# Loading k and q of the first 512 tokens by head halves, eight tokens to a partition, over two DMA rings

## The chip, the cores and the metric

The kernel runs on one core of a Trainium2 chip. The metric is the device time of one execution in microseconds (us). The core has TensorE (PE) with its weight loads (PEld), VectorE (DVE), ScalarE (ACT), GpSimd (POOL) and SyncE (SP). PE writes to PSUM alone; ACT and DVE empty PSUM; POOL works on SBUF. DMAs are put on a ring by the engine that issues them and run on 16 DMA engines.

## The reference

There are 8 sequences of 576 tokens, 8 heads of 64. Attention sees a band of 32 tokens on each side; its result is the input of a feed-forward network with a squared ReLU.

```
scores = (q @ k.T) / sqrt(64);  scores = where(|i - j| <= 32, scores, -1e9)
attn   = exp(scores - max) ;    attn = attn / (sum + 1e-9)
x      = (attn @ v), heads side by side, reshaped to (4608, 512)
h      = x @ w_in                      # 512 -> 2048
out    = (s * max(h, 0)**2 + b) @ w_out  # 2048 -> 512, float32
```

All inputs are float32. The kernel casts to bfloat16 ahead of the matmuls.

## The kernel before, in words

**Tiles.** The 4608 tokens are 36 tiles of 128. Tile j attends with its 128 queries as two halves of 64, each against 128 keys, so it needs key blocks j and j+1, where block j starts 32 tokens ahead of query tile j. The feed-forward part takes 8 tiles of 128 tokens and then 14 of 256: `s1` (L1114, x by w_in), a ReLU on ACT (L1124, sometimes DVE), a square on DVE (L1144), `s2` (L1178, by w_out), and an output step on DVE (L1187) that also adds the constant vector CVEC, which needs all of w_out (`cvec`, L1007: matmuls of L1011, a spread of L1023, a DVE step of L1028).

**How k and q come in, up to tile 13.** `load_pair` (L608) fetches 256 tokens of k or q in one DMA (two where a sequence ends inside): two tokens to a partition, all 8 heads, so that a contiguous piece is 2 x 64 floats, 512 bytes. K0 is a special case: it starts 32 tokens ahead of the data, so it has 112 partitions, and the first 16 are set to zero by a DVE memset (L462). `cast_pair` (L634) turns it to bfloat16 in KQN in two instructions of 128x512. `turn_pair` (L645) transposes it on PE in two groups of four 128x128 transposes into a PSUM bank (L653; profile names tp and ht) and then copies it to KQT, one copy of 128x512 for each tile (recorded as L597 on ACT, L592 on DVE, the lines of the helper `move`). v is loaded by `load` (L566) in pieces of 256 bytes. w_in and w_out are loaded by `load_w` (L536) in four parts each of 1 MB with pieces of 2 KB, into the buffer that later holds GT (so the profile calls it gt), and cast in four instructions each.

**Attention of one tile.** `attend` (L881): 16 score matmuls of 64 rows (L910) into the two banks SC; eight DVE instructions that add the mask and take the maximum (L920); eight exponentials on ACT (L927); the sum's reciprocal on DVE (L935, L938); eight scalings on ACT, DVE or POOL (L593, L598); transposes (L961, for tiles 0 to 3, on PE; by DMA from tile 4 on); the product with v (L983 and others), and a copy to XT.

**What sets the order.** Nothing is ordered by hand but the first loads. A planner (`_Plan.order`, L152) takes each instruction with a key (its due time, from the tile number plus the table RANK), a cost and its dependences, and lays them out on the five engines; it also chooses the engine where several may do it. What it gives is one fixed list for each engine, with semaphore waits. Where it sees PE idle for over 0.3 us in the opening, it puts in fill matmuls on a tile of ones (L500), whose results nobody reads. The constants START to TURN, PAIR and the cost arguments describe the chip to the planner; changing one changes the lists and not the computation. The first loads are listed by hand:

```
FIRST = "K0 Q0 v0 v1 K1 v2 Q1 v3 i0 i1 i2 i3|v4 K2 o0 o1 o2 o3 s0||"   # L68
```

K, Q: pairs; v: one tile; i, o: a quarter of w_in, w_out; s: the two scalars. The part behind the first bar is issued with tile 1. All of it goes by SyncE's ring, in this order; K2 waits for the casts of K0, whose buffer it uses, and each part of w_out for the casts of the w_in part in the same place.

Of the kernel before, what the change touches and what calls it, by code (L numbers as in the profile page):

```python
# [6 lines left out]
BF16 = mybir.dt.bfloat16  # L7
# [5 lines left out]
D = 64  # L13
H = 8
# [10 lines left out]
START, RAMP, RING, ISSUE, LAND, TURN = 800.0, 1200.0, 2700.0, 700.0, 1400.0, 300.0  # L25
# [8 lines left out]
    "av": (-1120, -880, -20, -160, 640, -880, 420, -3660, -2360, -760, 40, 180, 660, 80, -800),  # L34
    "ck": (0, 62940, 0, 63660, 200, 63640, -1120, 63760, 680, 61500, -240, -4080, 400, -3060, 740),
    "cq": (-680, -17980, -1560, -19380, -40, -16220, -760, -24200, -1480, -18720, -1600, -15700, -160, -16880, -740),
    "cs": (60, 460, -6260, -6260, -6260, -6260, -6260, -6260, -6260, -6260, -6260, -6260, -6260, -6260, 0),
    "cv": (-180, -1420, -740, -1220, -1380, -1880, -1340, -640, 4900, -1480, 5600, -300, -940, -420, -1000),
    "ex": (-480, 320, 440, -2400, -220, -240, 20, -180, -220, -1140, 1040, -160, 80, 100, -40),
    "kt": (-340, -29820, 40, -30840, 20, -29740, 2280, -30920, 2000, -31040, -1620, -31040, -3100, -30900, -240),  # L40
    "ktc": (2800, -1080, 820, -420, 300, -740, -200, 1680, 160, 200, -240, -940, 180, -680, 80),
    "ktd": (2020, 2020, 2020, 2020, 2020, 2020, 2020, 2020, 2020, -840, 1240, 100, -4360, -300, -12200),
    "mx": (-460, 100, -380, 0, 2760, -160, 4840, -500, 2280, -140, -80, 300, -640, 260, 3360),
    "no": (-1180, 1780, 200, -1160, 1500, 80, -460, -200, 160, 200, 20, 7880, 2680, -960, -180),
    "ou": (-20, 920, 0, 540, 1380, 920, 1040, 160, 540, -10560, -40, -4920, 560, -5040, 200),
    "pt": (-160, -180, 400, 900, -39920, -39920, -39920, -39920, -39920, -39920, -39920, -39920, -39940, -39940, -60),
    "ptc": (-80, 4280, 1920, -40, -20820, -20820, -20820, -20820, -20820, -20820, -20820, -20820, -21020, -21020, 0),
    "ptd": (70520, 70520, 70520, 70520, 1160, -440, -40, -220, -1960, -1320, -160, -200, -720, -400, -60),
    "qt": (-20, -580, -660, -1700, -80, -2220, -80, -2700, -300, 1000, -10980, 1000, -1240, 680, -320),
    "qtc": (500, 1220, 4440, -720, -20, -260, 740, -3260, -180, -300, -200, -120, 0, 320, 0),  # L50
    "rc": (-560, -720, 240, 180, 120, 500, -1220, -1380, -5320, -880, 300, -540, -3260, 640, 6120),
    "re": (460, 1700, -1680, -4400, -1680, -1760, -3280, 60, 20, -248640, -440, -255780, -480, -255860, -1260),
    "s1": (800, 1520, 420, 4120, -140, -60, -1100, 0, 1600, 12880, 140, 11300, -6540, 11520, -980),
    "s2": (-3780, -700, -20, 40, 1280, -1020, -240, -420, 100, 86620, -8420, 86900, -4240, 86820, 0),
    "sc": (100, 520, -2480, -80, -360, -400, -840, -100, 1400, -1700, -260, -580, -80, 1500, -4320),
    "sq": (360, -540, 1080, 280, 180, -1240, 5280, -160, -60, -1420, 200, 1500, 540, 1500, 780),
    "vo": (28460, 28360, 1180, 540, -80, 2920, 5080, -1540, 260, -80, -1260, 680, -620, -120, 2820),
    "wi": (1180, -11800, -11800, -11800, -11800, -11800, -11800, -11800, -11800, -11800, -11800, -11800, -11760, -11760, 0),
    "wo": (-960, 4060, 4060, 4060, 4060, 4060, 4060, 4060, 4060, 4060, 4060, 4060, 3720, 3720, 0),
    "xt": (840, 100, -100, -520, -1120, 420, -460, 1420, 100, -20, 120, -640, 580, -1000, -220),  # L60
# [5 lines left out]
NPM, SQPOOL, NWHOLE, NV = 0, 0, 4, 5  # L66
PAIR0, FORE, PTB = 16, 2, 5
FIRST = "K0 Q0 v0 v1 K1 v2 Q1 v3 i0 i1 i2 i3|v4 K2 o0 o1 o2 o3 s0||"  # L68
# [42 lines left out]
class _Plan:  # L111
# [40 lines left out]
    def order(self):  # L152
# [15 lines left out]
        dma_free = {"sp": RAMP, "act": 0.0}  # L168
# [15 lines left out]
        while len(out) < len(self.nodes):  # L184
# [65 lines left out]
            if n.dsem is None:  # L250
                end = free[e] + n.lat
            else:
                early, ring = t < STEADY, "act" if e == "act" else "sp"
                if e == "sp":
                    free[e] = room(free[e], n.ndesc)
                took = n.dtime * (1.0 if early else DSLOW)
                dma_free[ring] = max(dma_free[ring], free[e] + (ISSUE if early else n.iss)) + took
                if ring == "sp" and early:
                    dma_free[ring] += TURN if (n.ndesc == 512) != (kind == 512) else 0.0
                    kind = n.ndesc  # L260
                end = dma_free[ring] + (LAND if early else 1000.0)
                if e == "sp":
                    queue.append((dma_free[ring], took, n.ndesc))
                    del queue[:-12]
# [87 lines left out]
def bass_sliding_window_symmetric__then__act_starrelu_kernel(  # L352
# [41 lines left out]
    with ExitStack() as es:  # L394
# [39 lines left out]
        XQ = [sb((128, DM), BF16, "xq") for _ in range(2)]  # L434
        MB = {m: sb((128, 4, 128), BF16, "mb") for m in ("mm", "fm")}
# [22 lines left out]
        K0 = -1.0e6  # L458
        add("dve", lambda e: e.memset(ONES[:], 1.0), 150, K0, writes=["ONES"])
        add("dve", lambda e: e.memset(FLAT[:, 0, :], NEG), 100, K0, writes=[("FLAT", 0)])  # L460
        add("dve", lambda e: e.memset(FLAT[:, 1, :], 0.0), 100, K0, writes=[("FLAT", 1)])
        add("dve", lambda e: e.memset(KALL[0:16, 0:2 * DM], 0.0), 970, K0 + 10, writes=[("K32", 0, "lo")])  # L462
# [16 lines left out]
        if NPM:  # L479
            for m in ("mm", "fm"):  # L480
                add("pool" if m == "mm" else "act", lambda e, m=m: (e.tensor_copy if m == "mm" else e.copy)(
                    MB[m][:, :, :], mm[:, :].unsqueeze(1).broadcast_to((128, 4, 128))),
                    620 if m == "mm" else 550, KC + 2, reads=mids, writes=[("MB", m)])
            add("dve", lambda e: e.memset(MB["fm"][0:64, :, 0:32], NEG), 130, KC + 2, writes=[("MB", "fm")])
        for m, cuts in (("fm", ((0, 0),)), ("ml", ((1, 32),)), ("lf", ((0, 96), (1, 64)))):
            key = KC + 2 if m == "fm" and not NPM else -LEAD
# [23 lines left out]
        lastload = [None]  # L510
        wcnt = [0]
# [24 lines left out]
        def load_w(which, c):  # L536
            if which in WCAST:
# [6 lines left out]
                   else w_out[:, 4 * c:4 * c + 4, :])  # L544
            lastload[0] = add("sp", lambda e: [e.dma_start(w32, src)], 500, -LEAD - 900,
                              writes=[("W32", s_, g) for g in range(4)], dsem=f"dw{s_}",
                              dtime=2800, behind=lastload[0], ndesc=512)
# [18 lines left out]
        def load(src, t0, dst, name, key, sem, x):  # L566
            pcs = parts(t0)

            def fn(e):
                return [e.dma_start(dst[r:r + n, :].rearrange("p (h d) -> p h d", h=H),  # L570
                                    src[b, :, s0:s0 + n, :].rearrange("h s d -> s h d"))
                        for (b, s0, r, n) in pcs]
# [4 lines left out]
            lastload[0] = add("sp", fn, 640.0 * len(pcs), key, writes=[name], dsem=sem,  # L577
                              ndma=len(pcs), dtime=(1040.0 if x < 4 else 1330.0) * tot / 128, behind=lastload[0], ndesc=8 * tot,
                              after=hold + ([gate] if gate and gate.eng == "pe" else []))
            recent.append(lastload[0])  # L580
            if gate and gate.eng == "sp":
# [26 lines left out]
        def load_pair(what, J):  # L608
# [9 lines left out]
            def fn(e):  # L618
# [8 lines left out]
            lastload[0] = add("sp", fn, 640.0 * len(pcs), 128 * j - LEAD - 600, writes=[(nm, 2 * a), (nm, 2 * a + 1)],  # L627
                              dsem=f"d{what}{a}", ndma=len(pcs), dtime=PAIR * tot / 256, behind=lastload[0],
                              ndesc=4 * tot, after=hold + ([gate] if gate and gate.eng == "pe" else []))
            recent.append(lastload[0])  # L630
            if gate and gate.eng == "sp":
# [13 lines left out]
        def turn_pair(what, J):  # L645
# [13 lines left out]
            for x in range(2):  # L659
# [7 lines left out]
                     akey(j) - (128 if what == "K" else 0) + rank(ck_, j), [res], [("KT" if what == "K" else "QT", kt)],  # L667
                     scale=SCALE if what == "Q" and j < NPM else None, after=[first] if first else [])
# [29 lines left out]
        def k_turn(j):  # L698
            kn, kt = j % NB, j % NKT
            key = akey(j) - 128  # L700
            if j > KQDMA:
                add("sp", lambda e: [e.dma_start_transpose(KQT[kt][:, :, :], KQN[kn][:, :])],
                    1300, key + 64 + rank("ktd", j), reads=[("KN", kn), ("QN", kn)],
                    writes=[("KT", kt), ("QT", kt)], dsem=f"dkt{kt}", dtime=1270, ndesc=1024, iss=-316.0)
                return

            def fn(e):
                for pr in range(NPAIR):
# [5 lines left out]
                 key + rank("ktc", j), ["TP"], [("KT", kt)])  # L714
# [26 lines left out]

        def early(j):
            key = akey(j)
            ka, kb = j % NKT, (j + 1) % NKT
            va, vb = VE[j % NVE], VE[(j + 1) % NVE]
            vres = [("VE", j % NVE), ("VE", (j + 1) % NVE)]
            pb, mb, ptb, xq = j % NP, j % NM, j % NPT, j % 2
            kind = "fm" if 2 * j % UPB == 0 else "mm"
            assert kind == "fm" or (2 * j + 1) % UPB < UPB - 1 and 2 * j % UPB < UPB - 1

            def half(blk, pr, a):
                return ((NKT - 1 - blk) * 2 * NPAIR + pr) * 2 + a

            for hh in range(2):
                r0 = 64 * hh
                m = add("pe", lambda e, hh=hh: e.matmul(SC[hh][:, :, :], lhsT=IDENT[:, :], rhs=MB[kind][:, :, :],
                                                        start=True, stop=False),
                        214, key - 150 + rank("mk", j), reads=["IDENT", ("MB", kind)], writes=[("SC", hh)])

                def scores(e, hh=hh, r0=r0):  # L760
                    for pr in range(NPAIR):
                        for u in range(2):
                            c1, c2 = half(kb, pr, 0), half(ka, pr, 1)
                            for part in range(2 if u and c1 > c2 else 1):
                                dst = SC[hh][64 * u:64 * u + 64, pr, :]
                                if u == 0:
# [487 lines left out]
```

## Time and profile before

| | us |
|---|---|
| median of 3 runs (lowest, highest) | 319.09 (317.71, 319.47) |
| the profiled execution, its own time | 318.41 |
| its span, first to last instruction | 316.7 |
| PE busy in the span | 300.6 |
| of it, fill matmuls (L500), first 72 us | 13.35 |
| the first score matmul starts (tile 0) | 9.06 |
| casts of K0 / Q0 start | 4.99 / 7.03 |
| first cast of w_in / the first s1 matmul | 17.90 / 19.36 |
| cast of K2 | 31.78 |
| first cast of w_out / the first s2 matmul | 34.00 / 35.97 |
| matmuls for CVEC start (L1011) | 45.03 |

All times in the lower part are counted from the start of the span. The clock granted to TensorE was 1.00 throughout. A time in the table says when an instruction started; a cast starts when its DMA has landed, or later where the engine is busy.

How to read the rows that are shown further on. A row of the slices gives the busy share of an engine in each fortieth of the span, 7.9 us, in tenths. A row of the chain in order of time has start, length, engine, what was done, and how many. A row of the windows has the window, its length, the busy time and the number of instructions of each engine, the granted clock, the mean busy share of the 16 DMA engines (it can be over 1 where packets overlap), and GB/s.

### The profile page before, as it was taken

The page shows a single profiled execution, that of the slowest core. Times are in us where ns is not written, and L with a number is a line of the kernel's source. Part 1 is how long each engine was busy: PE and PEld are TensorE (multiplying, and loading weights), DVE is VectorE, ACT ScalarE, POOL GpSimd, SP SyncE. Part 2 cuts the span into 40 slices and gives each one's busy share as a digit, 9 for nine tenths or more (in the row PEclk, how much of TensorE's full clock was granted, in tenths as well). Part 3 has the DMA queues.
Part 4 walks back from the last instruction along what each step waited for, and adds up shares of the span by engine and source line. Part 5 has one row for each costly group of instructions (what it writes and reads, how often), then busy time and mean ns, then how long its engine had stood idle before and what let it go on. Part 6 is the DMA issues. An engine that isn't in the chain of part 4 may idle for free.

```text
span 316.7 us, 10629 instructions
## 1 busy us (share of the span) xinstructions
PE 300.6 (95%) x4057; PEld 212.7 (67%) x4095; DVE 214.0 (68%) x930; ACT 218.6 (69%) x767; POOL 181.4 (57%) x393
## 2 busy tenths in 40 slices
PE   6879899999999999999999999999999999999996
PEld 4567675677866776575767676666767585848664
DVE  4786866867977778368497766867777668534432
ACT  4898867988995879278577868686859587706230
POOL 3444455897879475925949676666766771700000
PEclk9999999999999999999999999999999999999999
DMA  8999999999999999996999999999999952310001
GB/s 187 289 404 273 393 193 237 234 212 246 189 169 246 233 180 239 226 224 159 192 181 243 207 198 229 195 203 196 222 193 219 183 135 70 85 51 33 35 35 66
DMA packets 165139, 60.99 MB, mean 193 GB/s; under 512 B 142048, under 2 KB 156512, under 8 KB 165088
## 3 DMA queue, kind: packets, MB, share of 16 engines
q1 hardware_dynamic: 165088, 60.31, 91.2%
q8 instruction: 32, 0.52, 0.7%
q14 instruction: 19, 0.16, 0.2%
HBM read 36.70 MB, written 9.44 MB: 146 GB/s over the span
## 4 chain that ended last, share of the span: by engine, by line
PE 81%; DMA 8%; SPq 4%; ACT 3%; issue 2%; DVE 1%; POOL 1%
PE ht L1114 27%; PE outp L1178 24%; PE tp L1178 10%; PE outp L1114 5%; PE tp L1114 4%; DMA gt<-in_moe_w_in_dram 3%; DMA k<-in_k_dram 3%; PE av L1178 2%; PE av L855 2%; DMA q<-in_q_dram 2%; SPq L619 2%; SPq L570 2%; PE sc L910 2%; PE av L725 2%; ACT p L927 1%
## 5 line engine op out<-in xcount | busy, mean ns | idle before, releaser
L593 POOL TENSOR_SCALAR p<-p,rc 128x128 bf16<-128x128 bf16 x271 | 111.2, 431 | 43.4 <-DVE rc L938 43.4
L927 ACT ACTIVATE p<-ss,mx 128x128 bf16<-128x128 f32 x288 | 111.9, 391 | 23.4 <-DVE mx L920 23.2
L1114 PE MATMUL ht<-xt,win 128*128 128x256 bf16 (+1 forms) x1144 | 109.3, 249 | 1.8 <-DVE mx L920 1.1
L1144 DVE TENSOR_TENSOR gt<-r 128x512 bf16<-128x512 bf16 x144 | 70.3, 490 | 50.6 <-ACT r L1124 48.8
L1114 PEld LDWEIGHTS ht<-xt,win 128*128 128x128 bf16 x1144 | 91.2, 98 | 17.0 <-POOL win L592 1.3
L1124 ACT ACTIVATE r<-ht 128x512 bf16<-128x512 f32 x109 | 64.5, 593 | 44.0 <-PE ht L1114 43.6
L1178 PE MATMUL outp<-wout,gt 128*128 128x512 bf16 (+1 forms) x358 | 83.1, 374 | 3.6 <-issue 2.1
L920 DVE CUSTOM_DVE_ANT_0 ss<-sc,mask 128x128 f32<-128x128 f32 x224 | 52.5, 282 | 12.3 <-PE sc L910 12.3
L1178 PEld LDWEIGHTS outp<-wout,gt 128*128 128x128 bf16 x384 | 35.7, 98 | 37.0 <-DVE cvec L1028 0.6
L927 ACT ACTIVATION_READ_ACCUMULATOR p<-ss,mx 128x1 f32 x288 | 54.4, 189 | 0.0
L1178 PE MATMUL tp<-wout,gt 128*128 128x512 bf16 x136 | 31.3, 379 | 0.9 <-issue 0.5
L592 POOL CAST ve<-v 128x512 bf16<-128x512 f32 x37 | 23.5, 636 | 13.2 <-DMA v<-in_v_dram 12.6
L592 POOL CAST kqn<-k 128x512 bf16<-128x512 f32 x33 | 20.4, 627 | 18.1 <-DMA k<-in_k_dram 18.0
L592 POOL CAST kqn<-q 128x512 bf16<-128x512 f32 x31 | 20.6, 672 | 10.5 <-DMA q<-in_q_dram 10.4
L1187 DVE SCALAR_TENSOR_TENSOR outs<-outp,scb,cvec 128x512 f32<-128x512 f32 (+1 forms) x24 | 17.7, 737 | 12.9 <-PE outp L1178 12.7
L1178 PEld LDWEIGHTS tp<-wout,gt 128*128 128x128 bf16 x144 | 13.6, 98 | 15.6 <-DVE gt L1144 0.2
L920 DVE DVE_READ_ACCUMULATOR2_ANT mx<- 128x1 f32 x288 | 23.4, 81 | 0.0
L592 DVE CAST xt<-av 128x512 bf16<-128x512 f32 (+1 forms) x34 | 22.2, 675 | 1.7 <-PE av L725 1.3
L1114 PE MATMUL outp<-xt,win 128*128 128x256 bf16 x144 | 18.7, 273 | 0.0
L1124 ACT ACTIVATE r<-outp 128x512 bf16<-128x512 f32 x18 | 10.7, 596 | 8.4 <-PE outp L1114 8.4
L1114 PEld LDWEIGHTS outp<-xt,win 128*128 128x128 bf16 x144 | 14.0, 98 | 2.6
L1114 PE MATMUL tp<-xt,win 128*128 128x256 bf16 x120 | 15.6, 273 | 0.0
(84 smaller groups left out, 252.0 us busy)
## 6 DMA issues: line engine op xcount, KB each, us to landing
out_dram<-outs SPq DMA_DIRECT2D x35, 256.0 KB, 2.6
v<-in_v_dram SPq DMA_DIRECT2D x28, 256.0 KB, 4.8
q<-in_q_dram SPq DMA_DIRECT2D x22, 256.0 KB, 4.6
k<-in_k_dram SPq DMA_DIRECT2D x18, 256.0 KB, 4.0
gt<-in_moe_w_in_dram SPq DMA_DIRECT2D x4, 1024.0 KB, 10.4
gt<-in_moe_w_out_dram SPq DMA_DIRECT2D x4, 1024.0 KB, 10.8
q<-in_q_dram SPq DMA_DIRECT2D x4, 512.0 KB, 6.3
v<-in_v_dram SPq DMA_DIRECT2D x8, 192.0 KB, 4.6
```

Source lines behind the costliest of these rows:

```text
L570: return [e.dma_start(dst[r:r + n, :].rearrange("p (h d) -> p h d", h=H), src[b, :, s0:s0 + n, :].rearrange("h s d -> s h d")) for (b, s0, ...
L592: return e.tensor_copy(dst, src)
L593: return e.tensor_scalar(dst, src, scale, 1.0, ALU.mult, ALU.mult)
L619: return [e.dma_start(big[r:r + n // 2, 2 * DM * a:2 * DM * a + 2 * DM].rearrange("p (h x) -> p h x", h=H), src[b, :, s0:s0 + n, :].rearra ...
L725: r = e.matmul(PA[64 * hh:64 * hh + 64, u, 64 * pr:64 * pr + 64], lhsT=vt[r0:r0 + 64, 128 * pr + 64 * hh:128 * pr + 64 * hh + 64], rhs=PTS ...
L920: lambda e, ss=ss, x=x, y=y: e.tensor_tensor_reduce(out=SS[ss][:, x, :], in0=banks[y % 2][0][:, y // 2, :], in1=MASK[kind][:, :], scale=-S ...
L927: lambda e, ss=ss, x=x, y=y: e.activation(P[pb][:, y, :], SS[ss][:, x, :], AF.Exp, bias=MX[mb][:, y:y + 1], scale=-1.0, accum_out=SM[mb][: ...
L1114: r = e.matmul(hbank[:, nt * f:nt * f + nt], lhsT=WIN[:, kc, 128 * ft:128 * ft + 128], rhs=XT[:, kc, x0:x0 + nt], start=(kc == 0), stop=(k ...
L1124: return e.activation(R1[rb][:, :], hbank[:, :], AF.Relu, bias=0.0, scale=1.0)
L1144: return e.tensor_tensor(d, r, r, ALU.mult)
L1178: r = e.matmul(op_[:, 0:cn], lhsT=GT[:, g_, fc, :], rhs=WOUT[:, fc, c0:c0 + cn], start=(fc == 0), stop=(fc == 15))
L1187: add("dve", lambda e, ob=ob, op_=op_, c0=c0, cn=cn: e.scalar_tensor_tensor(OUTS[ob][:, 0:cn], op_[:, 0:cn], SCB[:, 0:1], CVEC[:, c0:c0 + cn],
```

## The change

1. `load_oct`, `cast_oct` and `turn_oct` are new and take the place of K0, Q0, K1 and Q1. `load_oct(h)` loads heads 4h to 4h+3 of tokens 0 to 511: k into partitions 0 to 63 by SyncE's ring, q into partitions 64 to 127 by ScalarE's, eight tokens to a partition, in pieces of 8 x 64 floats, 2 KB. The buffers are the ones that held the pairs: QALL for X0, KALL for X1 (so the profile will call X0's k and q "q", and X1's "k"). K2 then waits for the casts of X1.
2. `cast_oct(h)` casts it in four instructions of 128x512, and `turn_oct(h)` transposes it in 32 transposes of 64 rows (k and q alternate, to the banks TP and HT[1]) and copies it out in eight copies of 128x256 (96 columns a head for the first block of k).
3. Tile 0's scores go in two parts, pairs 0 and 1 to SC, pairs 2 and 3 to the two banks PA, so that the first part needs X0 alone.
4. ScalarE issues its two loads ahead of the load of its function table, which is now an entry of the plan. The memset of 16x1024 of KALL gives way to one of 32 columns of KQT for four heads' pairs.
5. The RANK table is another one throughout, TURN is 400 for 300, w's `dtime` 2950 for 2800; so the planner's lists differ in the whole kernel.
6. Removed, as not used with NPM = 0: `early`, the tiles XQ and MB, and the variable NPM.

```diff
-FIRST = "K0 Q0 v0 v1 K1 v2 Q1 v3 i0 i1 i2 i3|v4 K2 o0 o1 o2 o3 s0||"
+PAIR0, FORE, PTB, OCT = 16, 2, 5, 1250.0
+FIRST = "X0 X1 v0 v1 v2 v3 i0 i1 i2 i3|v4 K2 o0 o1 o2 o3 s0||"
...
+        add("act", lambda e: e.add_instruction(mybir.InstLoadActFuncSet(
+            name=nc.get_next_instruction_name(), ins=[], outs=[], act_func_set_id=ACT_TABLE_SET_ID)),
+            1300, 1.5 * K0)
...
-        add("dve", lambda e: e.memset(KALL[0:16, 0:2 * DM], 0.0), 970, K0 + 10, writes=[("K32", 0, "lo")])
+        add("dve", lambda e: e.memset(KQT[0][:, 0:NPAIR, 0:32], 0.0), 100, K0 + 10, writes=["KTlo"])
...
+        O32 = [QALL[:, :], KALL[:, 0:4 * DM]]
+        def load_oct(h):
+            for eng, src, r in (("sp", k, 0), ("act", q, 64)):
+                def fn(e, src=src, r=r):
+                    return [e.dma_start(O32[h][r:r + 64, :].rearrange("p (h x) -> p h x", h=4),
+                                        src[0, 4 * h:4 * h + 4, 0:512, :].rearrange("h (p i) d -> p h (i d)", i=8))]
+                n = add(eng, fn, 400.0, -LEAD - 600 - (2e6 if eng == "act" else 0), writes=[("O32", h, r)],
+                        dsem=f"dx{h}{r}", dtime=OCT, behind=lastload[0] if eng == "sp" else None, ndesc=256)
...
+        def cast_oct(h):
+            src = O32[h].rearrange("p (h i d) -> p i h d", h=4, i=8)
+            for i in range(4):
+                d_ = 2 * h + i // 2
+                cast(ANY, src[:, 2 * i:2 * i + 2, :, :],
+                     [("O32", h, 0), ("O32", h, 64)] + [(("Q32", "K32")[h], x) for x in range(4)],
+                     KQN[d_][:, DM * (i % 2):DM * (i % 2) + DM].rearrange("p (i h d) -> p i h d", i=2, h=4),
+                     ("QN" if i % 2 else "KN", d_), akey(0) - 330 + h + rank("ck", h))
...
+        def turn_oct(h):
+            banks = ((bank(TPF), "TP"), (bank(HT[1]), ("HT", 1)))
+            for i in range(4):
+                def fn(e, i=i):
+                    for x in range(4):
+                        c = DM * (i % 2) + 128 * x
+                        for w in range(2):
+                            r0 = 64 * w
+                            r = e.transpose(banks[w][0][:, 4 * i + x, :], KQN[2 * h + i // 2][r0:r0 + 64, c:c + 128],
+                                            IDENT[r0:r0 + 64, r0:r0 + 64])
...
+                    ahead[w] = [move(
+                         ("act", "dve"), {"dve": 340.0, "act": 330.0},
+                         dst.rearrange("p g (t i) -> p g t i", i=8),
+                         banks[w][0][:, :, t0:t1].rearrange("p (i g) t -> p g t i", i=8),
...
-            n = add("pe", scores, 223, key + rank("sc", j), reads=[("KT", ka), ("KT", kb), ("QT", kb)],
-                    writes=[banks[0][1], banks[1][1]])
+            split = j == 0
+            def bank_of(y):
+                if split and y >= 4:
+                    return PA[:, y % 2, :].rearrange("p (a b) -> p a b", b=128), ("PTP", "AV")[y % 2]
+                return banks[y % 2]
+            for prs in ((0, 1), (2, 3)) if split else (range(NPAIR),):
```

## The prediction

> **What bounds the kernel now.** I read the page's busy shares first (PE 95%, every other engine under 70%), then the slices, the chain in order of time, and windows of the opening.
>
> ```profile
> PE 300.6 (95%) x4057; PEld 212.7 (67%) x4095; DVE 214.0 (68%) x930; ACT 218.6 (69%) x767; POOL 181.4 (57%) x393
> PE   6879899999999999999999999999999999999996
> DMA  8999999999999999996999999999999952310001
> ```
>
> From the sixth slice (39.6 us) on, PE is the bound; before it, PE is not full, and much of what it does is the warm-up fill of L500, which computes nothing: 13.35 us of fill in the first 72 us, none after 40. So the kernel is an opening of about 39 us in which useful work waits, then some 275 us of full PE. PE was busy 232.01 of the 236 us from 64 to 300. A change that touches the opening gains just what it moves the start of the full stretch.
>
> The chain in order of time shows what the opening waits for:
>
> ```profile
> 11.60 9.79 DMA gt<-in_moe_w_in_dram
> ...
> 23.13 8.60 DMA k<-in_k_dram
> 31.78 0.88 POOL kqn L592
> 32.66 0.05 issue
> 32.71 0.40 PE tp L653 x4
> ```
>
> w_in lands, then the third pair of k (K2, which is queued behind it), is cast and turned, and PE can go on. The w_out loads are queued behind K2. All of this is one SyncE ring, kept full: the windows give its rate by what it carries.
>
> ```profile
> 3.00:5.00 2.00, 1.91 (x12) 1.23 (x10) 0.93 (x9) 0.59 (x4) 0.00 (x0) 1.00 1.19 305
> 6.00:8.00 2.00, 0.94 (x11) 0.47 (x9) 0.43 (x1) 1.17 (x2) 0.86 (x1) 1.00 1.35 215
> 8.30:9.30 1.00, 0.87 (x23) 0.56 (x20) 0.00 (x0) 0.85 (x2) 0.65 (x2) 1.00 1.19 284
> 11.30:12.30 1.00, 0.73 (x11) 0.66 (x12) 0.93 (x5) 1.00 (x7) 0.46 (x2) 1.00 1.18 283
> 14.50:23.50 9.00, 7.14 (x110) 5.41 (x108) 7.58 (x48) 8.34 (x33) 4.36 (x8) 1.00 1.05 403
> 25.00:27.00 2.00, 1.79 (x34) 1.26 (x30) 1.43 (x6) 1.73 (x8) 1.28 (x2) 1.00 1.27 203
> ```
>
> The columns after the window and its length are PE, PEld, DVE, ACT, POOL, the clock, the DMA share and GB/s. In order: K0 and Q0 (512-byte packets) 305; v0 and v1 (256 bytes) 215; K1 284; Q1 283; w_in (2 KB packets) 403; K2's pieces of 48 and 80 partitions, with the end of v4, 203. The DMA share is at 1 throughout: bytes and packet size set when each load lands.
>
> **Part 1: the loads of k and q.** Removed are K0 (0.459 MB), Q0, K1 and Q1 (0.524 MB each): 2.03 MB at the mean of 305, 284 and 283, 291 GB/s, 6.98 us of the queue. Added are four of 0.524 MB, 2.097 MB in 2 KB packets. Their rate is not in the trace: no load there has 64 partitions, and none comes from ACT's ring. The bounds are the rows above. At w_in's 403 they take 5.20 us, 1.8 less. At the slowest, 203, they take 10.33 us, 3.3 more; at 283, as now, 7.41 us, 0.4 more. I take 403: packet size is what w_in shares with them, and k (partitions 0 to 63) and q (64 to 127) in flight together cover the 128 partitions that w_in covers. 203 was seen with 512-byte pieces of unequal size, of which one at a time was in front.
>
> The Trainium skill (SBUF — State Buffer, section "Can I just issue two DMAs to hit both halves?") speaks against this: it says that two concurrent DMAs at partitions 0 and 64 gave only 6% over a single one, and its table has 196 GB/s for partitions 0 to 63. By that rule I estimate 208 GB/s and 10.1 us, 3.1 more than now. K2's 203 agrees with it in size, w_in's 403 cannot tell. That is the rival on the slow side, below. The skill's DMA: Bandwidth & Descriptors (section on queues, rings and completion order) says each DMA engine takes packets of its queues in turn, which would mix k and q packet by packet; no row here shows it.
>
> Behind these loads the order on SyncE's ring is v0 to v3, the four w_in, v4, K2, w_out, s, as before with the pairs taken out. v0 to v3 stay 256-byte work. So w_in, K2, w_out all move 1.8 us ahead. SP issues six loads before w_in in place of eight, each with 256 to 1024 rows; it was held by the full ring, not by issuing (v4's issue took 7.65 us), so nothing is lost there.
>
> **Part 2: ACT's two issues.** They stand ahead of its table load (0.80 to 2.08). Two issues at 0.54 us (Q0's on SP) put the load to about 3.2 and the mask copies (now 2.89, waiting for POOL) to about 3.9; DVE's mask memsets follow 0.3 late. The first use is near 10 us. Cost nothing; the cover is over 5 us.
>
> **Part 3: casts, turns and copies of the first four tiles.** X0 (heads 0 to 3 of k and q) lands near 6.5: the queue had moved 0.18 MB by 3.0 us, the other 0.87 MB take 2.2 us, and Q0's landing lag was 1.35 us (data through near 5.7, cast at 7.03). X1 lands near 9.15. Eight casts become eight casts of the same size. 64 transposes of 64 rows take the place of 32 of 128: at 0.22 us per four (L653) they are at most 1.8 us more, on a PE that fills there; 8 fill matmuls go. 16 copies of 256 columns replace 8 of 512. Those on ACT were 0.59; a 128x256 copy from PSUM took 0.35 to 0.37, so 9 cost 3.2 us where 6 cost 3.5. DVE gets 7 at about 0.4 (2.8) for 2 at 0.68 (1.4), and loses one memset of 0.91 from its idle start.
>
> They come in one lump, and that costs. ACT's order up to the second x copy of tile 0 holds 2 casts at 0.62, 9 copies at 0.36, 15 exponentials at 0.385, 3 scalings at 0.39, one w_in cast 0.62 and 2 x copies at 0.36: 12.8 us. From 6.5, with 1.0 us idle for the first turns, that ends at 20.3. It ended at 18.72. The first FFN matmul is then at 20.4, not 19.36: 1.0 late, although w_in's first quarter lands at 16.1, not 17.9. DVE adds a wait: its X1 casts stand ahead of tile 0's first four maxima, which so start at about 10, not 9.53; queued behind is all of tile 0's softmax.
>
> But the next quarters have landed by then (18.7, 21.3, 23.9), and ACT and DVE no longer owe the copies of Q1 and K1. The second FFN group follows at about 21.8 (was 22.92), the third at 24.1 (27.13), the fourth at 26 (28.96), tile 1's first by 28 (30.43). Then PE's order has K2's transposes, as now: at 32.71 less 1.8, 30.9. The late start is hidden by nearly 3 us of that wait; without this cover it costs 1.0.
>
> **Part 4: from K2 on.** PE runs nine FFN groups before the first w_out matmuls, now seven; two groups of 0.89 fill what was waiting and fill (1.04 of L500 at 37.5, 0.22 of wait). But the constant vector needs all of w_out, whose last casts began at 42.66 on landing, and its matmuls (L1011, at 45.03) come at about 43.2. I count no gain beyond the 1.8 that w_out lands earlier. w_out's casts shift from DVE (8 to 4) to POOL (4 to 7), 0.62 to 0.87 each: three more, about 2.3 us, in 7 us where POOL was busy 3.11; hidden, at worst 0.9 for one cast too late.
>
> **Part 5: the rest.** Every order behind is re-planned: 3509 matmuls after the constant vector against 3505, 53 changes of tile shape against 55, the last 540 matmuls in the same order. PE's named waits from 64 us on are about 3 us, most of them 0.16 each ("issue"). I take 0, between 0.7 lost (the longest single wait behind 38.8 us) and 0.7 gained.
>
> **The sum.** -1.8 + 0 + 0 + 0 + 0 = -1.8 us. The profiled execution has a span of 316.7 and took 318.41, 1.7 around it; 318.41 - 1.8 = **316.6**. The median shown, 319.09, is 0.7 above that execution, so 317.3 counted from it is inside the range. The measurement tells from no change about 0.5%, 1.6 us: 317.5 to 320.7.
>
> **The rivals.**
> - *Forecast*, 316.6, with 315.0 to 317.6 as its own range: 0.55.
> - *The halves get in each other's way.* k fills one half of the partitions and q the other, and the 2 KB packets are held to the 203 of the K2 window. The place is 2 to 13 us; w_in, K2 and w_out land 3.3 later, and all behind: 321.7. It decides below 244 GB/s, where 2.097 MB take 1.6 us more than now. For it: K2's rate; against: two rings at once, which that window has not. This is the skill's rule as a mechanism; the trace bears it out only half. 0.12.
> - *The opening is held by ACT and DVE, not by DMA.* ACT was busy 8.34 of 9.00 us while w_in loaded. If exponentials and casts keep the lag of 1.0 us through to K2, w_out's early landing is used late: between -0.8 and +0.8, 318.4. Against: ACT and DVE were idle for 5 us and more between 24 and 36. 0.18.
> - *Packet size is not the limit* (the reading side is): 283 as now, +0.4, 318.8. Against: three kinds of packet, three rates, in the order of size. 0.08.
> - *The re-planned stretch moves on its own* by over 1.6, either way: 0.07.
>
> **How the numbers follow.** Faster by over 0.5%: nine tenths of the forecast, and half of the last case, 0.53. Slower: the halves, and the other half, 0.15. Same: the rest, 0.32. The range 315.0 to 319.6 takes in the first, third and fourth case (0.81); it leaves out 321.7.
>
> **What would show it.** Right: 390 GB/s or more from 3 to 7 us, w_in's first casts near 16.1, K2's near 30, w_out's near 32.2, and PE full from about 31. Wrong at step 1: about 200 or 285 GB/s there, w_in's casts at 17.9 or later. Wrong at step 3: w_in landed, but the third FFN group later than 26. Wrong at step 5: the gain is there at 45 us and gone at 300.

## The result, and the profile after

The change made the kernel slower: 320.49 us median of 20 runs, against 317.90 us for the kernel before in 20 runs beside it, a ratio of 1.0081 (95% interval 1.006 to 1.0103). The forecast was 316.6; the time lies outside the range, on the side of the rival in which the halves get in each other's way (321.7).

The profiled execution took 321.30 us with a span of 319.5 (before: 318.41 and 316.7). Its slices, from the page:

```profile
PE 305.7 (96%) x4119; PEld 212.9 (67%) x4119; DVE 214.5 (67%) x935; ACT 216.5 (68%) x767; POOL 181.1 (57%) x396
PE   5868998999999999999999999999999999999996
PEclk9599999999999999999999999999999999999999
DMA  7999999999999999999999999999899982420011
GB/s 166 228 381 283 397 239 211 231 254 198 211 158 209 226 219 203 210 226 203 236 166 257 183 199 194 211 215 215 198 209 184 172 163 51 110 57 35 28 40 66
```

PE is full from the sixth slice on, as before, but its first slice is emptier (5, was 6), and the clock falls in the second. The two PE totals can't be set against each other: records are missing from the trace of before (554 matmuls of the second FFN product there, 592 here).

The windows show the loads; after the window and its length the columns are PE, PEld, DVE, ACT, POOL, the granted clock, the DMA share and GB/s:

```profile
3.00:5.00 2.00, 2.00 (x12) 1.48 (x11) 0.34 (x4) 1.18 (x4) 0.00 (x0) 1.00 1.03 259
5.00:7.00 2.00, 0.29 (x3) 0.01 (x1) 0.00 (x0) 0.00 (x0) 0.00 (x0) 1.00 1.08 223
7.00:9.00 2.00, 0.44 (x16) 0.45 (x16) 0.93 (x2) 0.62 (x1) 0.87 (x1) 0.79 1.06 231
9.00:11.00 2.00, 1.84 (x36) 0.97 (x31) 1.03 (x3) 1.20 (x4) 0.00 (x0) 0.50 1.07 252
16.00:25.00 9.00, 6.28 (x108) 4.42 (x109) 7.61 (x46) 7.49 (x32) 4.36 (x8) 1.00 1.03 384
51.80:319.50 267.70, 264.38 (x3468) 182.08 (x3468) 179.39 (x786) 181.82 (x654) 156.92 (x347) 1.00 0.93 175
```

While X0 and X1 come in, the engines of the DMA are busy all the time (share 1.03 to 1.08) and move 223 to 259 GB/s; with w_in they move 384. PE, DVE, ACT and POOL have next to nothing to do from 5 to 8 us. The 1024 packets of 2 KB took 9.08 us from first to last, 231 GB/s, with a median of 154 ns for one packet. X0 was cast at 8.05 (forecast 6.5), X1 at 12.38 (9.15), w_in's first quarter at 20.57 (16.1; before 17.90).

The chain in order of time carries it on (start, duration, what):

```profile
12.73 7.81 DMA gt<-in_moe_w_in_dram
...
25.02 8.41 DMA k<-in_k_dram
33.46 0.62 ACT kqn L599
...
46.46 0.94 PE outp L980 x57
47.40 0.88 issue
48.28 0.29 PE outp L980 x7
...
51.78 3.63 PE outp L1156 x16
```

w_in and K2 are waited for as before, K2's cast at 33.46 instead of 31.78. Then the constant vector's 64 matmuls begin at 46.39, 1.4 us later than before (45.03), and stop for 0.88 us before the last seven. The last cast of w_out had ended at 46.11, and at 43.80 before. The first whole group of second FFN matmuls into outp (L1156, L1178 before) needs that vector. It starts at 51.78. The chain of the kernel before has this in its place:

```profile
47.89 0.75 DVE cvec L1028
...
48.92 3.42 PE outp L1178 x15
```

The record of the group's first matmul is missing there: its weight load is at 48.69, just behind the vector's end at 48.64. So the group is 3.1 us late. Most of that is the later start (1.4), the stop (0.9) and a group of four w_out matmuls that the new order puts behind the constant vector's (0.6). From the group to the end of the span it is 267.7 us here and 268.0 before. **The whole loss is made in the opening**, and next to nothing (0.3 us) is gained behind it.

The profile names nothing that PE waited for in the stop of 0.88 us, and all of w_out was cast by then. It ended 2.6 us after a 16 KB packet of the instruction queue had begun (45.66); whether PE waited for that isn't shown.

### The profile page after: what moved, and what is told of

The parts are those of the page before. It is cut to its first block, busy times and chain, and to the rows that moved or that the text cites. A ratio compares the mean times of both kernels' runs of the same rounds, so it can differ in the third digit from the quotient of the medians.

```text
span 319.5 us, 10737 instructions
## 1 busy us (share of the span) xinstructions
PE 305.7 (96%) x4119; PEld 212.9 (67%) x4119; DVE 214.5 (67%) x935; ACT 216.5 (68%) x767; POOL 181.1 (57%) x396
## 4 chain that ended last, share of the span: by engine, by line
PE 86%; DMA 5%; SPq 4%; DVE 2%; ACT 2%; issue 1%
PE ht L1092 29%; PE outp L1156 26%; PE tp L1156 10%; PE outp L1092 5%; PE tp L1092 4%; SPq L568 3%; PE av L1156 3%; DMA k<-in_k_dram 3%; DMA gt<-in_moe_w_in_dram 2%; PE av L815 2%; PE sc L868 2%; PE av L783 2%; PE tp L660 1%; PE sc L1156 1%; ACT p L896 1%; PE ht L868 1%
## 5 line engine op out<-in xcount | busy, mean ns | idle before, releaser
L595 POOL TENSOR_SCALAR p<-p,rc 128x128 bf16<-128x128 bf16 x271 | 108.0, 416 | 43.5 <-DVE rc L907 43.5
L1156 PE MATMUL outp<-wout,gt 128*128 128x512 bf16 (+1 forms) x384 | 88.1, 375 | 0.9 <-DVE cvec L997 0.5
L1102 ACT ACTIVATE r<-ht 128x512 bf16<-128x512 f32 x105 | 61.9, 593 | 39.8 <-PE ht L1092 39.2
L1156 PEld LDWEIGHTS outp<-wout,gt 128*128 128x128 bf16 x384 | 36.2, 98 | 38.0 <-DVE gt L1122 1.0
L889 DVE CUSTOM_DVE_ANT_0 ss<-sc,mask 128x128 f32<-128x128 f32 x220 | 51.1, 282 | 9.5 <-PE sc L868 8.1
L1156 PE MATMUL tp<-wout,gt 128*128 128x512 bf16 x144 | 33.1, 379 | 0.0
L594 POOL CAST ve<-v 128x512 bf16<-128x512 f32 x37 | 24.3, 657 | 11.1 <-DMA v<-in_v_dram 10.8
L594 POOL CAST kqn<-k 128x512 bf16<-128x512 f32 x33 | 21.4, 653 | 15.4 <-DMA k<-in_k_dram 15.3
L594 POOL CAST kqn<-q 128x512 bf16<-128x512 f32 x31 | 20.4, 662 | 13.8 <-DMA q<-in_q_dram 8.6
L1156 PEld LDWEIGHTS tp<-wout,gt 128*128 128x128 bf16 x144 | 13.7, 98 | 15.5
L594 DVE CAST xt<-av 128x512 bf16<-128x512 f32 (+1 forms) x36 | 22.9, 659 | 0.3 <-PE av L952 0.3
```

The lines of the kernel that those rows point to most:

```text
L594: return e.tensor_copy(dst, src)
L595: return e.tensor_scalar(dst, src, scale, 1.0, ALU.mult, ALU.mult)
L889: lambda e, ss=ss, x=x, y=y: e.tensor_tensor_reduce(out=SS[ss][:, x, :], in0=bank_of(y)[0][:, y // 2, :], in1=MASK[kind][:, :], scale=-SCA ...
L1102: return e.activation(R1[rb][:, :], hbank[:, :], AF.Relu, bias=0.0, scale=1.0)
L1156: r = e.matmul(op_[:, 0:cn], lhsT=GT[:, g_, fc, :], rhs=WOUT[:, fc, c0:c0 + cn], start=(fc == 0), stop=(fc == 15))
```

## The experiments

The theories put to the runs, as the expectations call them: **H** (half), a load that writes half of the partitions moves at about half rate, and a load of the other half beside it doesn't make up for it; **R**, the two rings hinder each other; **S**, pieces of 2 KB out of k and q are read slowly; **C**, the clock that fell to 0.50 costs the time. In five kernels only the X loads or their rings differ (e1, e2, e5, e7, e9): every engine works in the changed kernel's order, but for the loads themselves. So the rest of the plan has no part in what they show.

**e1_all128: each load over all 128 partitions.** Same rings, bytes and 2 KB pieces; the data lie elsewhere, so the first 512 tokens' values are not those of the reference.

```
-  O32[h][r:r + 64, :]             ... src[0, 4 * h:4 * h + 4, 0:512, :] ... "h (p i) d -> p h (i d)", i=8
+  flat = src ... "b h s d -> (b h s d)" ... [131072 * h:131072 * h + 131072]
+  O32[h][:, 16 * r:16 * r + 1024] ... flat ... "(h p x) -> p h x", h=2, p=128
```

A load takes 131072 consecutive floats, two pieces of 2 KB to a partition.

> Same two rings, same bytes, same 2 KB packets, but each of the four loads writes all 128 partitions (two pieces to a partition) instead of 64; k and q of the first tiles get other values of the same tensors, so the output of the first 512 tokens is not the reference's. Theory H (a load that writes one half of the partitions moves at about half the rate, and the two rings do not make up for it): 380 to 405 GB/s for the first 2.1 MB, first cast of w_in near 16 us (20.57 in the changed kernel), span 4 to 5 us shorter than the changed kernel's, so 1 to 2.5 below the kernel before. Theory R (SyncE's and ScalarE's rings hold each other up): the rate stays at 215 to 240 GB/s and the time at that of the changed kernel. Theory S (2 KB pieces of k and q are read slowly): the same as R.

Measured: 317.83 us median, ratio 0.9999 (0.9976 to 1.0023) to the kernel before. Its windows and chain:

```profile
5.00:7.00 2.00, 1.15 (x20) 0.50 (x18) 0.94 (x2) 0.62 (x1) 0.86 (x1) 1.00 1.00 376
47.60:315.00 267.40, 264.34 (x3468) 181.72 (x3468) 179.82 (x786) 181.78 (x654) 158.21 (x348) 1.00 0.97 175
```

```profile
43.40 1.01 PE outp L981 x64
...
47.61 3.63 PE outp L1157 x16
```

376 GB/s where the changed kernel had 223, a median packet of 84 ns where it had 154, and the group of second FFN matmuls at 47.61, 4.2 us ahead of the changed kernel. R falls, as the rings are the same, and S as far as the size of the pieces goes. But the number of partitions and the half changed together, and so did the place that is read; the kernel with even and odd partitions, below, takes them apart. Against the kernel before nothing is gained, to which I come back.

**e2_onering: q's loads on SyncE's ring too.**

```
-            for eng, src, r in (("sp", k, 0), ("act", q, 64)):
+            for eng, src, r in (("sp", k, 0), ("sp", q, 64)):
```

> q's two loads go by SyncE's ring too, in the order k, q, k, q; partitions and packets as in the changed kernel. H: 210 to 220 GB/s, the time within 0.7 us of the changed kernel, as two rings gained nothing. R: 380 GB/s or more and 4 us faster.

Measured: 320.82 us, ratio 1.008 (1.005 to 1.011); X in 9.43 us, 222 GB/s. One ring is as slow as two: R falls again, and ACT's ring brings nothing as long as each load keeps to a half.

**e3_warm: 44 initial fill matmuls in place of 14.**

```
-        add("pe", lambda e: fill(e, "attn", 14), 2990, K0, reads=["ONES"]).tag = "attn"
+        add("pe", lambda e: fill(e, "attn", 44), 2990, K0, reads=["ONES"]).tag = "attn"
```

> 30 more fill matmuls at the start, so that PE does not pause from 5.3 to 8.6 us and the granted clock (0.50 from 8.5 to 14.5 us in the changed kernel) stays at 1.00. Theory C (the dropped clock costs the time): 2 us or more faster than the changed kernel. H: at most 0.5 us, since w_in's landing decides and does not move.

Measured: 320.67 us, ratio 1.0075 (1.005 to 1.01). The clock row of its page:

```profile
PEclk9998999999999999999999999999999999999999
```

The dip of the second slice is gone and the loss is still there: C falls. PE waits for data there, at whatever clock.

**e5_mix: finer turns.** One ring, eight loads of 256 KB (two heads each), k and q in turn.

```
+            for a in range(2):
+                for src, r in ((k, 0), (q, 64)):
...
+                        e.dma_start(O32[h][r:r + 64, 1024 * a:1024 * a + 1024] ...
```

> The changed kernel with the eight loads of X on one ring, two heads each, k and q in turn, 256 KB each, still 64 partitions to a load; nothing else is changed. Tells whether finer turns between the two halves lift the rate. Theory half: a load is slow while its half alone is written, and a ring works its loads nearly one after another, so 215 to 270 GB/s and 320 to 321 us. Rival mix (the halves only collide because they came in bulk, 512 KB of one and then 512 KB of the other): 300 GB/s and more, first w_in cast under 19, 318 to 319 us.

Measured: 321.52 us in one run (before, beside it: 318.42), X in 9.43 us, 222 GB/s.

```profile
5.00:7.00 2.00, 0.22 (x3) 0.00 (x0) 0.00 (x0) 0.00 (x0) 0.00 (x0) 1.00 1.07 228
```

Finer turns don't lift the rate, as theory half says.

**e7_comb: the same 64 partitions' worth, but every second partition.** k on the even and q on the odd partitions; the rest still reads halves, so the first 512 tokens are computed from mixed-up rows.

```
-                    O32[h][r:r + 64, :]
+                    O32[h][r // 64:128:2, :]
```

> The changed kernel with k on the even and q on the odd partitions instead of 0..63 and 64..127; rings, bytes, 2 KB pieces, order of every engine unchanged; the values of the first 512 tokens come out wrong, since the rest still reads the halves. Tells whether the number of partitions or the half that a load is kept to sets its rate. Theory half (the lower or upper 64 partitions take only part of the rate, whichever load it is): each load now reaches over all of the memory, X loads at 350 to 400 GB/s, first w_in cast near 17.2, about 317.8 us. Theory count (64 partitions, wherever they lie, take half the rate): 215 to 260 GB/s as in the changed kernel, first w_in cast 20 to 21, about 320.5 us.

Measured: 319.22 us, ratio 1.0028 (1.0011 to 1.0045).

```profile
3.00:5.00 2.00, 2.00 (x11) 1.45 (x10) 0.34 (x4) 1.19 (x4) 0.00 (x0) 1.00 0.99 347
5.00:7.00 2.00, 0.68 (x7) 0.21 (x7) 0.53 (x2) 0.54 (x1) 0.49 (x1) 1.00 1.04 402
```

402 GB/s with 64 partitions to a load. **It is the reach of the load over the partitions, not their number.** The source, the pieces and the rings are the changed kernel's, so S falls here too. From 4.7 to 5.4 us nearly only k's ring moved packets (136 of 137), one load on 64 partitions by itself, at 398 GB/s. The Trainium skill (SBUF — State Buffer, section "Can I just issue two DMAs to hit both halves?") says that the ports are chosen by the partition span of a single transfer, that two transfers are not joined, and that only one that spans all 128 partitions uses all ports. The runs agree: from 5 to 7 us loads kept to halves moved 223 GB/s (228 in e2_onering and e5_mix), and the same number of partitions spread out 402. The median time is higher than the rate lets expect (317.8); its profiled run, with 317.63, was the fastest of its ten. Why is open.

**e4_quads: a version that computes everything at full reach.** Four tokens to a partition (1 KB pieces), each load on 128 partitions, 32 transposes of 128 rows in place of 64 of 64; the planner is told so.

```
-  O32[h][r:r + 64, :]            ... "h (p i) d -> p h (i d)", i=8
+  O32[h][:, 16 * r:16 * r + 1024] ... "h (p i) d -> p h (i d)", i=4
-  add("pe", fn, 160, ..., writes=[banks[0][1], banks[1][1]]).mode = 4
+  add("pe", fn, 240, ..., writes=[banks[w][1]])
```

> Four tokens to a partition instead of eight: each load of k or q (four heads of 512 tokens) writes 128 partitions in 1 KB packets, k from SyncE's and q from ScalarE's ring; 32 transposes of 128 rows. H: above 283 GB/s (512-byte packets on 128 partitions) and below 403 (2 KB): the 2.1 MB take 5.2 to 7.4 us, and the time is 3 to 5 us below the changed kernel, 0 to 2 below the kernel before. R: 215 to 240 GB/s and no faster than the changed kernel.

Measured: 333.37 us, ratio 1.0484 (1.0457 to 1.0512), a miss. The loads were as fast as expected (344 to 387 GB/s, X0 cast at 6.34), and the time was lost far behind them, as the chain shows:

```profile
62.85 8.16 POOL p L595 x22
71.01 0.91 SPq L920
71.96 3.26 DMA pts<-p
75.27 0.46 PE av L780 x14
```

POOL works off 22 scalings in a row (8.16 us), a transpose by DMA waits for them, and PE for the transpose. Changed costs had given another plan; whether that was all, the next kernel tells.

**e6_quads_held: the same loads in the changed kernel's order.** Costs and dependences given to the planner as in the changed kernel.

```
-  add("pe", fn, 240, ..., writes=[banks[w][1]])
+  add("pe", fn, 160, ..., writes=[banks[0][1], banks[1][1]]).mode = 4
-  [("O32", h, 64 * w)]
+  [("O32", h, 0), ("O32", h, 64)]
```

> The same loads as in the four-tokens-to-a-partition kernel (1 KB pieces, every load on 128 partitions), computing everything, but with the costs and dependencies that the planner is told set to those of the changed kernel, so that every engine's order is the changed kernel's (only the pairs of 64-row transposes become one transpose of 128 rows). Theory A (the 1 KB loads are as good as the 2 KB loads on 128 partitions, and the 13 us that were lost mid-kernel came from the planner's other order): X loads at 340 to 390 GB/s, first w_in cast near 17.3, 317 to 318.5 us, no hole between 58 and 75 us. Theory B (something in the loads or the 128-row transposes themselves costs the 13 us): above 325 us again.

Measured: 318.48 us, ratio 0.9986 (0.9965 to 1.0008). The window of the lost time in the two kernels, first with the new plan, then with the order held:

```profile
55.00:75.00 20.00, 13.78 (x213) 9.18 (x212) 14.51 (x89) 15.76 (x70) 15.04 (x38) 0.90 0.52 117
```

```profile
55.00:75.00 20.00, 19.92 (x320) 14.35 (x319) 17.39 (x85) 18.14 (x72) 17.89 (x41) 1.00 1.07 219
```

PE has 13.78 us of work in these 20 us with the one plan and 19.92 with the other. The plan cost the 15 us between the two, not the loads. This kernel computes everything, is some 3 us ahead of the changed kernel by the two ratios (1.0081 - 0.9986), and cannot be told from the kernel before.

**e9_all128_onering: one ring at full reach.** e1_all128 with q's loads on SyncE's ring (the edit of e2_onering).

> The kernel whose four loads of X reach over all 128 partitions (2 KB pieces), with q's two loads issued on SyncE's ring behind k's instead of on ScalarE's; the first 512 tokens' values come out wrong as in that kernel. With the loads kept to halves the second ring had gained nothing. Theory span (only the reach of a load sets its rate, a ring more adds nothing): X loads at 350 to 400 GB/s again, first w_in cast 17 to 17.5, 317.3 to 318.4 us. Rival rings (at full reach two rings do help each other): 300 GB/s or less, first w_in cast after 18.5, above 318.8 us.

Measured: 319.72 us median, ratio 1.0055 (1.0029 to 1.0081), first w_in cast at 19.41. Neither theory holds whole. The ring moves 311 to 410 GB/s from 2.5 to 4.5 us and 360 to 393 from 6.5 to 8, as theory span says, but has a hole between:

```profile
5.00:6.00 1.00, 0.70 (x4) 0.16 (x2) 0.10 (x1) 0.11 (x1) 0.07 (x1) 1.00 0.39 115
```

The DMA share is 0.39 there: for most of that microsecond the DMA engines had no packets. With two rings (e1_all128) there was no hole: 348 to 397 GB/s from 4.5 to 6. What makes it isn't shown; SyncE had put in all four X loads by 2.8 us. By the two ratios (1.0055 - 0.9999), which were taken beside different runs of the kernel before, the second ring is worth some 1.8 us at full reach, and nothing with halves. Not all of the 1.8 need be the hole: in the profiled execution PE also stopped for 1.78 us inside the constant vector's matmuls, again with nothing named that it waited for, and again until 2.6 us after a 16 KB packet of the instruction queue (45.90).

**e10_all128_fill: does the clock eat the gain of e1_all128?** 1.6 times the fill matmuls in PE's waits of the opening; the first 512 tokens as in e1_all128.

```
-                    n.pre = (self.stage, int(FILL_SHARE * (t - free[e])
+                    n.pre = (self.stage, int(1.6 * FILL_SHARE * (t - free[e])
```

> The kernel whose loads of X reach over all 128 partitions, with 1.6 times the fill matmuls that the planner puts into TensorE's waits of the opening; nothing else is moved, and the first 512 tokens' values come out wrong as there. That kernel had its loads at full rate and yet was no faster than the kernel before; its granted clock fell to 0.5 from 20 to 23 us, when TensorE was at full work. Theory clock (that stretch eats the gain of the loads): the clock stays at 1.0, first x16 group of the second FFN matmuls near 46.5, ratio to before 0.993 to 0.997. Theory elsewhere (the gain isn't eaten by the clock): ratio 0.998 to 1.001 whatever the clock does. Fills that stand in the way would make it slower than 1.001.

Measured: 317.04 us, ratio 0.9977 (0.9956 to 0.9997). e1_all128, then this kernel:

```profile
20.00:22.00 2.00, 1.95 (x21) 1.64 (x22) 1.74 (x11) 2.00 (x10) 1.12 (x2) 0.50 1.05 407
```

```profile
20.00:22.00 2.00, 1.94 (x37) 1.66 (x37) 1.93 (x11) 2.00 (x9) 1.34 (x2) 1.00 1.05 405
```

The clock stays at 1.00, yet the group of second FFN matmuls starts at 47.64, as with the dip (47.61), not at 46.5. By that milestone the clock isn't what limits. The ratio lies between the ranges of the two theories (up to 0.997, from 0.998), and its interval overlaps that of e1_all128; whether the fills bring 0.7 us is not settled.

**e11_quads_fill: the same edit on e6_quads_held.**

> The kernel that computes everything with four tokens to a partition, each load on 128 partitions, in the changed kernel's order, with 1.6 times the fill matmuls in TensorE's waits of the opening; a candidate to beat both. Its clock was 1.0 already, so theory clock expects nothing of the fills here: 0.997 to 1.000 of the kernel before; if fills stand in the way of the chain, above 1.001.

Measured: 318.73 us, ratio 1.0024 (1.0006 to 1.0042), the group at 49.12 instead of 48.50: the range that the expectation gave for fills that stand in the way. No gain, so no version that computes everything beat the kernel before.

## Why the prediction was wrong, by its steps

**Part 1, the loads: this step failed.** The term was -1.8, from 403 GB/s; measured were 231 GB/s over the X loads, 9.08 us in place of 5.20. The trace had both rows, 403 (128 partitions, 2 KB) and 203 (K2's pieces of 48 and 80 partitions, 512 bytes), and I put the difference down to packet size. But Q1's row, 283, had 128 partitions and the same 512 bytes as K2: between those two it was not K2's packet size that differed (the end of v4, in 256 bytes, was in K2's window too). I also took it that k in one half and q in the other cover what w_in covers. e1_all128 and e7_comb show that they don't: the same packets on the same rings take 84 ns instead of 154 once each load reaches over both halves. The changed kernel's X loads took 2.6 us longer than those of e1_all128 (9.08, 6.45), and by the two ratios it is 2.6 us slower (1.0081 - 0.9999). Mixing hardly helps: from 7.8 to 10.3 us, when both rings moved packets, the mean was 252 GB/s, against 229 from 4.3 to 6.5, when nearly only SyncE's did. The Trainium skill's rule (SBUF — State Buffer, section "Can I just issue two DMAs to hit both halves?") was the right one; the 208 GB/s that the prediction worked out from it was 10% under the 231 measured.

**The rival was right in mechanism, and its size is in part luck.** It gave +3.3 and 321.7, with the point of decision at 244 GB/s; the profiled execution is +2.9, the medians +2.6. But its price was worked out at 203. At the 231 measured the loads are 2.1 us longer than before (9.08 against 6.98), and w_out's last quarter was cast 1.8 us later (44.42, 42.66). In the profiled execution the new order (0.6) and the stop (0.9), which the rival did not count, brought the loss up to its figure.

**Part 1, the sentence on turns.** The Trainium skill (DMA: Bandwidth & Descriptors, section "Queues, rings and completion order") has each DMA engine take packets in turn from the queues that it has work for. In the changed kernel they came in bulk: only ACT's ring until 4.3 us, only SyncE's from 4.5 to 6.7, then ACT's, and both together from 7.8 to 10.2. In e1_all128 both moved in every half microsecond from 2.5 to 8. The second agrees with the page; whether both queues had work for the engines in the changed kernel's first 7.8 us, the trace doesn't tell. The loss doesn't hang on it, as e2_onering and e5_mix show.

**At full rate the loads gain what was forecast, and the time doesn't.** In e1_all128 the X loads took 6.45 us, not 5.20: they moved 127 GB/s from 2.0 to 2.5 us and 283 from 2.5 to 3.0, a start that rows of the running queue left out. Yet the second quarter of w_in was cast 1.7 us ahead of before (19.74, 21.41), K2 2.1 (29.69, 31.78) and the last quarter of w_out 1.7 (40.95, 42.66). Only w_in's first quarter gained less, 0.7 (17.21, 17.90). Each load ends in 16 packets of 4 bytes; of that quarter's, 15 came from 14.80 to 15.73 and the last at 16.83, where before all 16 came from 16.35 to 16.98. What held up the last isn't shown; a 16 KB packet of the instruction queue, 1.31 us long, fell into that quarter (12.51), and before behind it (16.98).

The group of second FFN matmuls then started 1.1 us earlier than before (47.61, 48.69), and the medians don't show even that. The stretch from that group to the end was 267.4 us in e1_all128, 268.0 in e6_quads_held, 268.5 in e7_comb and 269.3 in e10_all128_fill (268.0 before, 267.7 after), so it moves by more than the gain from one execution to the next. Between -1.4 and +0.7 us, by the intervals of e1_all128 and e10_all128_fill, is all that can be said.

**Part 2** holds: ACT's issues took 0.70 and 0.63 us (0.54 taken), the table load ended at 3.48 (forecast 3.2), the mask copies began at 3.50, and what ACT waited for next was X0, until 8.05.

**Part 3**: in the changed kernel X was late, so its cover wasn't put to the test; the first FFN matmul came at 24.29 (forecast 20.4, before 19.36). At full rate, in e1_all128, it came at 21.0, and the cover was not enough: K2 was cast at 29.69, 2.1 us ahead of before, but PE turned it at 31.68, only 1.0 ahead of before (32.71). PE had been waiting for K2 then (0.97 us); now it was busy with FFN groups that stood ahead and came later than forecast: the third at 25.43 (24.1), the fourth at 28.25 (26), tile 1's first at 30.77 (28). Half of the gain at K2 ended there. That is the lag that the third rival described, with 318.4; but it did not last, for the constant vector's matmuls began 1.7 us ahead of before.

**Part 4** took w_out's landing as what the constant vector waits for. In the new order that holds: its matmuls began 0.28 us after the last cast of w_out had ended, at 46.39 in the changed kernel (46.11) and at 43.33 in e1_all128 (43.05; forecast 43.2). In the kernel before they began 1.2 us after it (45.03, 43.80), when PE had worked off the groups that stood ahead of them. From their start to the group behind it is 4.28 us in e1_all128 where it was 3.66, a loss of 0.6 by the new order. The part counted neither.

**Part 5** holds: 0 taken, 0.3 us gained from the group to the end of the span. That the plan could cost far more was in no rival; e4_quads shows 15 us from one.

## What to carry to other kernels

Before loads are split or joined, ask of each one which partitions it reaches over: two loads in flight, each kept to one half, ran here at 231 GB/s together, and the same bytes, on the same two rings, at 325 with every load over all 128 partitions (first packet to last). A rate is read from a row that shares all of the new load's properties, and where the two nearest rows differ in more than one, the difference belongs to neither until a run tells them apart. Where a planner lays out the work, hold its order while a load is tried; a plan of its own cost 15 us here, over five times the 2.6 us that the change itself cost.

## What the runs showed of the hardware

- Loads on every second partition (64 of them) ran at 393 to 418 GB/s from 4 to 7.5 us, as fast as loads on 128; on the lower or upper 64, from 4 to 11 us in the changed kernel, at 213 to 258 but for one half microsecond (315).
- Pieces of 1 KB on 128 partitions moved 341 to 389 GB/s from 4 to 8 us (46 ns a packet, the median), against 348 to 397 for 2 KB (84 ns) in e1_all128. With the 283 to 305 of 512-byte pieces in the kernel before, most of what larger pieces bring is had at 1 KB.
- The granted clock fell to 0.50 at about 8.1 us, when PE had stood idle since 5.3, and was back at 1.00 by 15; in e1_all128 it was at 0.50 from 20.0 to 23.4. Neither dip cost time that a run could show.
